# A delta rule, a routed and a dense feed-forward layer in one kernel: fillers by length, low parts on VectorE, one conversion step on ScalarE

## The chip, the cores and the metric

The kernel runs on one core of a Trainium2 chip. The metric is the device time of one execution in microseconds; of three runs of the kernel before the median counts. Engine names in rows: PE is TensorE (PEld its weight loads), DVE is VectorE, ACT is ScalarE, POOL is GpSimd, SP is SyncE, which only issues transfers here.

## What is computed

Three layers follow each other. All sizes are fixed: 4 batches, 8 heads, 768 steps, head size 48; 3072 tokens of 384; 8 experts with 1024 hidden units; a last layer with 2048.

```python
for t in range(S):                       # delta rule, per batch and head
    y[:, :, t] = einsum('bhd,bhde->bhe', q[:, :, t], state)
    v_old = einsum('bhde,bhd->bhe', state, kt)          # kt: normalised key
    state = state + bt * einsum('bhd,bhe->bhde', kt, vt - v_old)
...
h = np.maximum(x[mask] @ w1[e], 0.0)     # tokens of expert e (argmax of cosine logits)
out[mask] = gate_w[mask, None] * (h @ w2[e])
...
h = np.maximum(x @ w_in, 0.0)            # last layer; weights arrive in float64
return (h * h @ w_out)
```

## The kernel before

**Delta rule.** The sequence is cut into 24 steps of 32 positions (`NS`, `C`), four steps to a group. Within a step the recurrence is solved as a triangular system: `gram` multiplies keys with keys on TensorE, and `lanes` (line 191) lists the operations that invert the 32x32 systems of one group on VectorE: a transposition `turned` of 128x1024, a Newton iteration for the norms, factors, `scale`, 31 pairs `mul` and `acc` (lines 263 and 271), and a transposition `end` into `TTl[g]`. The list comes in stages of operations with a cost each, where an operation may cost zero. `Stream` holds one group's list and `fill` hands out its operations three times a step, by cost left and time to the step that needs them, so that VectorE works on later groups between the two `blocks` (line 321) that each step itself needs there: `Ub` and `Wb`. A step runs `mmV`, `mm1K`, `U`, then `W`, then `dS` for the next state; `mm1Q` stands behind `W` in steps 0 to 14 and ahead of it from 15 on, and `gram` of a later step ahead of `W`. In the prologue the first group's solve is interleaved with the first operations of the second group's. `warm(n)` runs n matmuls of 128 columns that write an unused bank. Engines take their instructions in program order, each for itself.

**Experts.** TensorE multiplies in a form with three matmuls: a float32 operand is split into a high part that TensorE's format holds and a low part that remains, and high x high, high x low and low x high are summed (`mm3`, lines 1088 to 1090). Expert e's first layer runs over eight blocks `fb` into three banks in turn (`P1`); ScalarE writes the high part `hh` of the result, VectorE the low part `hl` (line 1139), which frees the bank. The second layer runs over four token tiles in the order 0, 3, 1, 2; ScalarE scales them into `y` (line 1178), for tile 3 VectorE adds two halves (line 1180), and GpSimd stores the rows by an indirect transfer into `x2` (`to_x2`, line 1181), with row numbers that it reads from `xe`. After each block and each tile `run(k, ng, nw)` issues what else is due: `weights` splits the next pieces of weights (`split`, line 576: ScalarE rounds the high part, line 573; VectorE subtracts for the low part in the first ten pieces, GpSimd in nearly all later ones), `ng` operations of `gate` (norm, exponential, reciprocal), and `nw` operations of the queue `q64`. There are ten pieces to an expert: four over 768 columns of its second layer, then six over 512 of the next expert's first; expert 7's six are over 768.

**Conversion.** `q64` holds 28 pieces (12 over 512 columns, 16 over 384) of seven operations each from `w64`: the last layer's float64 weights are read as pairs of 32-bit words and made float32 by integer operations on VectorE (lines 1043 to 1057 and 1046), and each piece is stored into a scratch in DRAM, `wscr`, on SP's queue (line 1047). The last layer loads them back and splits them.

**Last layer.** Eight blocks of 384 tokens, on TensorE throughout.

## Time and profile before

| | us |
|---|---|
| three runs | 1028.61, 1035.83, 1039.15 |
| median | 1035.83 |
| profiled execution, its own time | 1029.11 |
| its span, first to last instruction | 1027.1 |

| stage | from | to | length |
|---|---|---|---|
| prologue | 0 | 52.09 | 52.09 |
| delta steps 0 to 19 | 52.09 | 249.71 | 197.62 |
| steps 20 to 23, last routing | 249.71 | 297.53 | 47.82 |
| expert 0 | 297.53 | 332.37 | 34.84 |
| experts 1 to 7 | 332.37 | 603.80 | 271.43 |
| first block of the last layer, to its last transposition | 603.80 | 637.54 | 33.74 |
| rest of the last layer | 637.54 | 1027.10 | 389.56 |

The stages were set by first matmuls of lines on TensorE. PEclk in a row is the granted clock as a share of 2.4 GHz. A busy VectorE may be one that works or one whose instruction stands; the length of single instructions of one form tells these apart.

### The profile page before, as it was taken

What the parts mean: (1) busy time and instruction counts of PE and PEld (TensorE: products, weight loads), DVE (VectorE), ACT (ScalarE), POOL (GpSimd) and SP (SyncE); (2) the same over time, 40 slices, a digit from 0 to 9 for tenths busy, and PEclk for the clock granted to TensorE, in tenths of its full rate; (3) what the DMA queues carried; (4) which work ended last, traced back from release to release, by engine and by line L of the source; (5) the groups of instructions that cost most, each with busy time, mean ns of one, the idle gap of its engine ahead of it and who ended that gap; (6) DMA issues with size and microseconds to landing.
All of it is one profiled execution on the core that took longest, in us unless ns stands there. A gap on an engine that the chain in (4) does not pass through costs nothing.

```text
span 1027.1 us, 22831 instructions
## 1 busy us (share of the span) xinstructions
PE 936.3 (91%) x9278; PEld 843.4 (82%) x9278; DVE 680.6 (66%) x1563; ACT 431.2 (42%) x1023; POOL 200.5 (20%) x176
## 2 busy tenths in 40 slices
PE   6688889799889889889889799999999999999998
PEld 5576667666677778678768788999999999999998
DVE  6789899998566999999999948160606060606060
ACT  2246566566624443443442446150505050505050
POOL 2000020112321464464464542000000000000000
PEclk9879898899989899999998999999999999999999
DMA  8558442241235663663673453101010000000000
GB/s 312 160 178 265 155 155 92 90 137 62 67 108 181 211 226 123 211 225 127 213 229 114 167 167 114 38 9 35 12 33 14 28 20 28 19 28 20 24 1 24
DMA packets 55443, 113.61 MB, mean 111 GB/s; under 512 B 5955, under 2 KB 34090, under 8 KB 55328
## 3 DMA queue, kind: packets, MB, share of 16 engines
q1 hardware_dynamic: 47600, 96.18, 28.7%
q0 software_dynamic: 3456, 9.59, 2.6%
q10 hardware_dynamic: 4272, 6.28, 1.9%
q8 instruction: 75, 1.23, 0.5%
q14 instruction: 40, 0.33, 0.1%
HBM read 82.02 MB, written 30.79 MB: 110 GB/s over the span
## 4 chain that ended last, share of the span: by engine, by line
PE 48%; DVE 14%; issue 2%; ACT 1%; DMA 1%; POOL 0%; SPq 0%; POOLq 0%; ACTq 0%; DVEq 0%
PE gp L1088 7%; PE gp L1090 7%; PE gp L1089 7%; PE xp L1088 4%; PE xp L1090 4%; PE xp L1089 4%; PE yp L1088 2%; PE yp L1089 2%; PE sp L1088 2%; PE yp L1090 2%; PE sp L1089 2%; PE sp L1090 2%; DVE t2k L1053 2%; DVE t2k L1051 1%; DVE gsm L83 1%
## 5 line engine op out<-in xcount | busy, mean ns | idle before, releaser
L1237 DVE TENSOR_TENSOR t4k<-t2k 128x384 f32<-128x384 f32 x128 | 77.3, 604 | 235.8 <-ACT t2k L1236 234.8
L263 DVE TENSOR_TENSOR tmp<-AL,TL 128x112 f32<-128x112 f32 (+15 forms) x186 | 62.0, 339 | 2.6
L271 DVE TENSOR_TENSOR TL<-TL,tmp 128x112 f32<-128x112 f32 (+15 forms) x186 | 61.7, 338 | 2.6
L1088 PE MATMUL gp<-wb,hh 128*128 128x384 f32 x184 | 63.2, 344 | 0.0
L369 ACT ACTIVATE Sb<-sp 48x384 f32<-48x384 f32 x92 | 44.7, 485 | 43.1 <-PE sp L359 41.6
L1090 PE MATMUL gp<-wb,hl 128*128 128x384 f32 x184 | 62.2, 338 | 0.3 <-DVE hl L1139 0.3
L1089 PE MATMUL gp<-wb,hh 128*128 128x384 f32 x184 | 62.1, 338 | 0.0
L1088 PE MATMUL gp<-xh,W 128*128 128x384 f32 (+1 forms) x153 | 53.8, 352 | 5.3 <-DVE hl L1139 5.0
L1088 PE MATMUL sp<-xh,W 128*128 128x384 f32 (+1 forms) x150 | 53.0, 353 | 4.7 <-DVE hl L1139 3.2
L1088 PE MATMUL yp<-xh,W 128*128 128x384 f32 (+1 forms) x153 | 52.8, 345 | 3.6 <-DVE hl L1139 3.3
L1181 POOL DMA_INDIRECT x<-y,xe x32 | 35.2, 1099 | 105.2 <-ACT y L1178 44.8
L485 POOL DMA_INDIRECT xs<-XG,sloti x24 | 26.8, 1118 | 146.9 <-ACT Ub L331 53.0
L1089 PE MATMUL gp<-xl,W 128*128 128x384 f32 (+1 forms) x153 | 53.4, 349 | 0.0
L1090 PE MATMUL gp<-xh,W 128*128 128x384 f32 (+1 forms) x153 | 53.3, 348 | 0.0
L1089 PE MATMUL yp<-xl,W 128*128 128x384 f32 (+1 forms) x153 | 52.7, 344 | 0.2 <-DVE xl L924 0.2
L1090 PE MATMUL yp<-xh,W 128*128 128x384 f32 (+1 forms) x153 | 52.6, 344 | 0.0
L1089 PE MATMUL sp<-xl,W 128*128 128x384 f32 (+1 forms) x150 | 52.4, 349 | 0.0
L1090 PE MATMUL sp<-xh,W 128*128 128x384 f32 (+1 forms) x150 | 52.3, 348 | 0.0
L1088 PE MATMUL xp<-wb,hh 128*128 128x384 f32 x152 | 51.6, 340 | 0.0
L1089 PE MATMUL xp<-wb,hh 128*128 128x384 f32 x152 | 51.3, 338 | 0.0
L1090 PE MATMUL xp<-wb,hl 128*128 128x384 f32 x152 | 51.3, 338 | 0.0
L359 PE MATMUL sp<-Wb,kL 128*48 128x96 f32 x736 | 45.5, 275 | 2.4 <-issue 1.0
(317 smaller groups left out, 2671.2 us busy)
## 6 DMA issues: line engine op xcount, KB each, us to landing
W<-in_moe_w_dram SPq DMA_DIRECT2D x42, 256.0 KB
W<-in_kq_dram SPq DMA_DIRECT2D x20, 512.0 KB
hb<-in_moe_w_dram SPq DMA_DIRECT2D x24, 384.0 KB
t4k<-in_moe_w_in_dram SPq DMA_DIRECT2D x12, 512.0 KB
t4k<-in_moe_w_out_dram SPq DMA_DIRECT2D x16, 384.0 KB
W<-wscr SPq DMA_DIRECT2D x16, 384.0 KB
xs<-padrow ACTq DMA_DIRECT2D x8, 693.0 KB
xe<-xs SPq DMA_DIRECT2D x8, 594.0 KB
```

The lines of the kernel that those rows point to most:

```text
L83: ops.append(lambda: V.scalar_tensor_tensor(t, t, -0.5, y, ALU.mult, ALU.mult))
L263: V.tensor_tensor(tv[0], AL[:, j, j + 1 :].unsqueeze(1).broadcast_to([128, n, m]), T[:, :n, j : j + 1].broadcast_to([128, n, m]), ALU.mult,)
L271: V.tensor_tensor(T[:, : j + 1, j + 1 :], T[:, : j + 1, j + 1 :], tv[0], ALU.add)
L359: PE.matmul(SP_[hq][64 * par : 64 * par + D, b * 96 : b * 96 + 96], kL2[g][:, i, b * 2 + hq], Wb[hq].rearrange("p b (m r) e -> p b r m e", ...
L369: A.activation(Sb[hq][r : r + D, :, :, par, :], SP_[hq][r : r + D, 0:384].rearrange("p (b m e) -> p b m e", b=4, m=2), AF.Copy,)
L485: G.indirect_dma_start(out=xs, out_offset=bass.IndirectOffsetOnAxis(ap=si[:, i : i + 1].bitcast(U32), axis=0), in_=XG[g][:, i0 + i, :], in ...
L1053: lambda: V.scalar_tensor_tensor(v["a"], u.bitcast(U32), float(0x70200000), v["a"], ALU.is_ge, ALU.mult),
L1088: PE.matmul(ps, hs, rh, start=first, stop=False)
L1089: PE.matmul(ps, hs, rl, start=False, stop=False)
L1090: PE.matmul(ps, ls, rh, start=False, stop=last)
L1181: to_x2 = lambda e=e, n=n, t=t, y=y: G.indirect_dma_start(out=x2, out_offset=bass.IndirectOffsetOnAxis(ap=xe[e][:n, t, XT : XT + 1].bitcas ...
L1237: V.tensor_tensor(s2, r, r, ALU.mult)
```

## The change

In the delta rule: each operation costs 0.075 us and its elements over 960, each transposition is split into four of 128x256 at a cost of 0.55, and a stream is one list without stages. `fill` gives each of the first two streams its due by the length left and the time left. The first solve runs alone; the second stream starts with step 0. `mm1Q` always stands ahead of `W`, `gram` behind it, the four masks of group 0 behind `W` of step 0, and the shares of the three fillers are 0.25, 0.4 and 0.35. `warm` matmuls are 512 columns wide and fewer: 29 in place of 146 before the loop, 10 in place of 55 in step 0, 2 in place of 10 in steps 1 to 3.

In the experts: every low part goes to VectorE. Conversion has six operations: the shift of line 1052 goes, the comparison uses an absolute value that ScalarE makes in place, and comes last. Its store goes to GpSimd's queue. Fewer conversion operations are popped (5 in the eight blocks of experts 1 to 6 in place of 8, and 6, 6, 4 at the tiles in place of 7, 7, 6; for expert 0 6, 6, 4 in place of 5, 5, 4). The exponential in `gate` is padded with empty operations so that it starts a group of four and its reader comes in the next. Row numbers are copied to a tile `rows` of their own.

```diff
-def add(f, n=C, gap=0.12):
-    ops.append((0.065 + n / 960 + gap if n else 0.0, f))
+def add(f, n=C, c=None):
+    ops.append((0.075 + n / 960 if c is None else c, f))
-def turned():
-    V.transpose(AL, GPs[g].rearrange("p s h j -> p j (s h)"))
+def turned(j):
+    V.transpose(AL[:, j : j + 8], GPs[g][:, :, :, j : j + 8].rearrange("p s h j -> p j (s h)"))
+
+def turn():
+    for j in range(0, C, 8):
+        add(lambda j=j: turned(j), c=0.55)
...
-    first, ops = ops, []
-    add(turned, C * C)
+    turn()
...
-    add(turned, C * C)
+    ops.append((0.0, begin))
+    turn()
-    for n, o in enumerate(nw):
-        add(o, C if n < 2 else 0)
-    first, ops = ops, []
+    for o in nw:
+        add(o)
...
-def end():
-    TTl[g] = wp.tile([128, C, C], F32, name="TTt", bufs=2)
+def end(i):
+    if i == 0:
+        TTl[g] = wp.tile([128, C, C], F32, name="TTt", bufs=2)
+    V.transpose(
+        TTl[g].rearrange("p u i -> p i u")[:, i : i + 8], T.rearrange("p c i -> p i c")[:, i : i + 8]
+    )
...
-if g == 0:
-    for u in range(1, 4):
-        ops.append((0.0, lambda u=u: vh(u)))
-third, ops = ops, []
-if g:
-    ops, third = third, ops
-add(end, C * C)
-return [o for o in (first, second, third, ops) if o]
+            add(lambda u=u: masked(g, u), 256)
+for i in range(0, C, 8):
+    add(lambda i=i: end(i), c=0.55)
+return ops
-    split(wbuf[i], c, raw.shape[1], raw, A, V if nstep < 10 or nstep > 78 and nstep % 2 else G)
+    split(wbuf[i], c, raw.shape[1], raw, A, V)
...
-        c, f = self.stages[0].popleft()
+        c, f = self.ops.popleft()
-        return c
+        self.due -= c
-    streams[:] = [st for st in streams if st.stages]
-    act = [[st, st.left / max((4 * st.g - now) / part, 1), len(st.stages)] for st in streams[:2]]
-    if len(act) == 2:
-        act[1][1] = min(act[1][1], max(1.2 * part, 4 * part - act[0][1]))
-    while act or route_q:
-        for a in act:
-            a[1] -= a[0].pop()
-        act = [a for a in act if a[1] > 0 and len(a[0].stages) == a[2]]
+    streams[:] = [st for st in streams if st.ops]
+    for st in streams[:2]:
+        st.due += st.left * min(1.0, part / max(4 * st.g - now, part))
+    while True:
+        act = [st for st in streams[:2] if st.ops and st.due > 0]
+        for st in act:
+            st.pop()
         if route_q:
             route_q.popleft()()
-    streams[:] = [st for st in streams if st.stages]
+        elif not act:
+            break
-        PE.matmul(YP[:, :128], ones, tri, start=True, stop=True)
+        PE.matmul(YP, ones, tri.unsqueeze(1).broadcast_to([128, 4, 128]), start=True, stop=True)
-warm(34)
+warm(9)
-grams(0, 1, 0, 4, 9)
+grams(0, 1, 0, 4, 0)
-while len(st0.stages) > 2:
+for _ in range(26):
...
-grams(1, 2, 0, 4, 9)
+warm(4)
+grams(1, 2, 0, 4, 2)
-grams(0, 2, 4, 8, 5)
+grams(0, 2, 4, 8, 1)
...
-nxt = Stream(1)
-nn = 0
-while len(st0.stages) > 2 or len(st0.stages) == 2 and len(st0.stages[0]) > 28:
+while st0.ops:
     st0.pop()
-while st0.stages:
-    st0.pop()
-    if len(nxt.stages) > 2 and nn % 3 == 0:
-        nxt.pop()
-    nn += 1
-grams(0, 2, 8, 12, 5)
+grams(0, 2, 8, 12, 1)
 drain(route_q)
-streams.append(nxt)
-for b in range(4):
-    masked(0, b)
+streams.append(Stream(1))
...
-    fill(s, 0.2)
+    fill(s, 0.25)
+    if s < 4:
+        warm(2 if s else 10)
+    mm1Q(s)
     if s > 0:
         xT = xrt(s - 1)
-    early = s >= 15
+    while g not in TTl or streams and streams[0].g == g and streams[0].ops:
+        streams[0].pop()
+    W(s, 0)
+    W(s, 1)
+    if s == 0:
+        for b in range(4):
+            masked(0, b)
     if ahead < min(15 if s < 4 else NS, s + 12):
-        early = False
         gram(ahead)
         ahead += 1
-    if early:
-        mm1Q(s)
-    while g not in TTl:
-        streams[0].pop()
-    if s < 4:
-        warm(10 if s else 55)
-    W(s, 0)
-    W(s, 1)
     if scats:
-    fill(s + 0.2, 0.4)
+    fill(s + 0.25, 0.4)
...
-    if not early:
-        mm1Q(s)
...
-        streams[-1].pop()
-    fill(s + 0.6, 0.4)
+    fill(s + 0.65, 0.35)
...
+ops.extend([lambda: None] * (-(len(ops) + 1) % 4))
 add(lambda: A.activation(lg, lg, AF.Exp))
+ops.extend([lambda: None] * 3)
...
+def top():
+
+    V.scalar_tensor_tensor(v["ai"], v["h"], -0x40000000, ui, ALU.bitwise_and, ALU.bitwise_or)
+
+def low():
+
+    V.scalar_tensor_tensor(u, v["l"].bitcast(U32), 2.0**-52, u, ALU.mult, ALU.mult)
+    A.activation(v["h"].bitcast(F32), v["h"], AF.Abs)
+
 def end():
-    V.tensor_tensor(v["a"], v["a"], u, ALU.add)
-    nc.sync.dma_start(wscr[i][:, c * n : (c + 1) * n], v["a"])
+    V.scalar_tensor_tensor(v["a"], v["h"].bitcast(F32), float(0x38100000), v["a"], ALU.is_ge, ALU.mult)
+    nc.gpsimd.dma_start(wscr[i][:, c * n : (c + 1) * n], v["a"])
 return [
     begin,
-    lambda: V.scalar_tensor_tensor(v["ai"], v["h"], -0x40000000, ui, ALU.bitwise_and, ALU.bitwise_or),
-    lambda: V.tensor_scalar(ui, v["h"], 1, None, ALU.logical_shift_left),
-    lambda: V.scalar_tensor_tensor(
-        v["a"], u.bitcast(U32), float(0x70200000), v["a"], ALU.is_ge, ALU.mult
-    ),
+    top,
     lambda: V.tensor_scalar(ui, v["ai"], -0x800000, None, ALU.bitwise_and),
-    lambda: V.scalar_tensor_tensor(u, v["l"].bitcast(U32), 2.0**-52, u, ALU.mult, ALU.mult),
+    low,
+    lambda: V.tensor_tensor(v["a"], v["a"], u, ALU.add),
     end,
...
+    rows_e = mp.tile([128, 4], I32, name="rows", bufs=2)
+    gops.insert(0, lambda e=e, rows_e=rows_e: V.tensor_copy(rows_e, xe[e][:, :, XT].bitcast(I32)))
...
-            run(fb + 1, 4, 2 if e + 1 == E else 1)
+            run(fb + 1, 4, 2 if e + 1 == E else (1, 1, 0, 1, 0, 1, 0, 1)[fb])
...
-            out_offset=bass.IndirectOffsetOnAxis(ap=xe[e][:n, t, XT : XT + 1].bitcast(U32), axis=0),
+            out_offset=bass.IndirectOffsetOnAxis(ap=rows_e[:n, t : t + 1].bitcast(U32), axis=0),
...
-        run(9 + i, 0, (7, 7, 6, 0)[i] if e else (5, 5, 4, 0)[i])
+        run(9 + i, 0, (6, 6, 4, 0)[i])
```

## Rows read from the trace of the kernel before

**Rows 1.** Busy time by stage: us from:to, length, then each engine; PEclk; DMA.

```profile
52.09:249.71 197.62, 171.94 (x3727) 134.80 (x3726) 184.03 (x580) 115.83 (x326) 23.39 (x28) 0.89 0.43 142
...
297.53:332.37 34.84, 32.85 (x173) 28.55 (x174) 24.77 (x59) 17.09 (x35) 2.56 (x2) 1.00 0.62 199
332.37:603.80 271.43, 241.04 (x1193) 207.52 (x1193) 249.55 (x411) 116.13 (x236) 141.77 (x98) 0.94 0.57 183
603.80:637.54 33.74, 31.49 (x176) 29.36 (x177) 25.26 (x37) 20.11 (x42) 9.68 (x6) 1.00 0.46 149
637.54:1027.10 389.56, 385.98 (x2223) 385.44 (x2221) 131.35 (x253) 125.52 (x276) 1.90 (x1) 1.00 0.07 22
```

**Rows 2.** Waits from 332.37 to 603.80 us: who <- whom: us, times, longest.

```profile
PE gp L1088 <- DVE hl L1139: 12.6, 3, 5.0
...
PE yp L1088 <- DVE hl L1139: 9.0, 4, 5.3
...
PE sp L1088 <- DVE hl L1139: 7.4, 3, 3.2
```

**Rows 3.** Timelines of VectorE and GpSimd in expert 4: start, length, what.

```profile
450.16 0.36 DVE L1056 TENSOR_SCALAR W<-t2k 128x384 int32<-128x384 int32 x1
450.56 0.56 DVE L1057 SCALAR_TENSOR_TENSOR W<-t4k,W 128x384 f32<-128x384 uint32 x1
451.15 2.01 DVE L1046 TENSOR_TENSOR t2k<-t2k,W 128x384 f32<-128x384 f32 x1
...
457.64 1.75 DVE L81 TENSOR_TENSOR gsm<-gsm 128x4 f32<-128x4 f32 x1
...
463.38 0.16 DVE L83 SCALAR_TENSOR_TENSOR gsm<-gsm 128x4 f32<-128x4 f32 x1
...
450.21 1.18 POOL L1181 DMA_INDIRECT x<-y,xe  x1 [1.89 <-ACT y L1178]
451.42 1.32 POOL L576 TENSOR_TENSOR W<-W 128x512 fp32r<-128x512 f32 x1
455.35 5.78 POOL L576 TENSOR_TENSOR W<-hb,W 128x768 fp32r<-128x768 f32 x3 [2.62 <-ACT W L573]
```

**Rows 4.** Line 576 alone, busy time in the same stretch: DVE, then POOL.

```profile
332.37:603.80 271.43, 1.29 (x2) 111.01 (x69) 0.94 0.57 183
```

**Rows 5.** VectorE's groups in expert 0: xcount | busy, mean ns | idle before.

```profile
L576 DVE TENSOR_TENSOR W<-hb,W 128x768 fp32r<-128x768 f32 x3 | 2.9, 955 | 1.2 <-ACT W L573 1.1
L576 DVE TENSOR_TENSOR wb<-W,wb 128x512 fp32r<-128x512 f32 x4 | 2.6, 689 | 1.3 <-ACT wb L573 1.2
...
L924 DVE TENSOR_TENSOR W<-ch,W 128x448 fp32r<-128x448 f32 x2 | 1.2, 620 | 3.0 <-ACT W L923 3.0
...
L1052 DVE TENSOR_SCALAR W<-t4k 128x512 int32<-128x512 int32 x2 | 0.9, 426 | 0.1
...
L1057 DVE SCALAR_TENSOR_TENSOR W<-t4k,W 128x512 f32<-128x512 uint32 x1 | 0.7, 684 | 0.0
```

**Rows 6.** Line 1181, the indirect stores of `y`: from issue to landing.

```profile
DMA to landing us min/median/max: 2.0/3.4/7.2
```

**Rows 7.** Timeline of VectorE, prologue and step 0.

```profile
40.17 1.95 DVE L203 STREAM_TRANSPOSE AL<-GPs 128x1024 f32<-128x1024 f32 x1 [4.25 <-ACT GPs L173]
...
53.95 1.43 DVE L188 TENSOR_TENSOR PL<-PL,mask 128x256 f32<-128x256 f32 x4
55.26 0.99 DVE L321 TENSOR_TENSOR Ub<-ch,blk 128x768 f32<-128x768 f32 x1
```

**Rows 8.** Timeline of TensorE, prologue and step 0.

```profile
15.02 0.43 PE L153 MATMUL sp<-W 64*32 64x32 f32 x21 [2.79 <-issue]
...
21.77 0.68 PE L153 MATMUL ch<-W 64*32 64x32 f32 x40 [2.98 <-issue]
...
55.11 4.08 PE L680 MATMUL yp<-tri,ones 128*128 128x128 bf16 x55
```

**Rows 9.** Waits from 332.37 to 603.80 us, GpSimd's longest on ScalarE's rounding.

```profile
POOL W L576 <- ACT W L573: 29.9, 10, 5.4
```

More of the change, by code (lines that the diff above doesn't have):

```diff
@@ L219, in factors @@
             add(lambda: V.reciprocal(r, nl))
-            add(lambda: V.tensor_tensor(r, r, r, ALU.mult), 0)
-            add(lambda: V.tensor_tensor(gam, r, betaL[:, g], ALU.mult), 0)
-            add(lambda: V.tensor_scalar(t1, gam, -1.0, None, ALU.mult), 0)
+            add(lambda: V.tensor_tensor(r, r, r, ALU.mult))
+            add(lambda: V.tensor_tensor(gam, r, betaL[:, g], ALU.mult))
+            add(lambda: V.tensor_scalar(t1, gam, -1.0, None, ALU.mult))
         nw = []
@@ L271, in acc @@
             V.tensor_tensor(T[:, : j + 1, j + 1 :], T[:, : j + 1, j + 1 :], tv[0], ALU.add)
-        def end():
-            TTl[g] = wp.tile([128, C, C], F32, name="TTt", bufs=2)
-            V.transpose(TTl[g].rearrange("p u i -> p i u"), T.rearrange("p c i -> p i c"))
-        v_steps = (23, 25, 27, 29) if g else (23,)
+        def end(i):
[4 more added lines that the diff above has]
+            )
         for j in range(31):
             for f in (mul, acc):
-                add(lambda f=f, j=j: f(j), (31 - j) * (j + 1), 0.02)
-            if j in v_steps:
-                u = v_steps.index(j)
-                add(lambda u=u: vh(u), 384, 0.02)
+                add(lambda f=f, j=j: f(j), (31 - j) * (j + 1))
+            if j in (23, 25, 27, 29):
+                u = (j - 23) // 2
+                add(lambda u=u: vh(u), 384)
                 if g:
-                    add(lambda u=u: masked(g, u), 256, 0.02)
-        if g == 0:
-            for u in range(1, 4):
-                ops.append((0.0, lambda u=u: vh(u)))
-        third, ops = ops, []
-        if g:
-            ops, third = third, ops
-        add(end, C * C)
-        return [o for o in (first, second, third, ops) if o]
+                    add(lambda u=u: masked(g, u), 256)
+        for i in range(0, C, 8):
+            add(lambda i=i: end(i), c=0.55)
+        return ops
     def mmV(s, hq):
@@ L648, in __init__ @@
             def __init__(self, g):
-                self.g, self.stages = g, [deque(ops) for ops in lanes(g)]
-                self.left = sum(c for ops in self.stages for c, _ in ops)
+                self.g, self.ops = g, deque(lanes(g))
+                self.left, self.due = sum(c for c, _ in self.ops), 0.0
             def pop(self):
-                c, f = self.stages[0].popleft()
+                c, f = self.ops.popleft()
                 f()
                 self.left -= c
-                if not self.stages[0]:
-                    self.stages.pop(0)
-                return c
+                self.due -= c
         def fill(now, part):
-            streams[:] = [st for st in streams if st.stages]
-            act = [[st, st.left / max((4 * st.g - now) / part, 1), len(st.stages)] for st in streams[:2]]
-            if len(act) == 2:
-                act[1][1] = min(act[1][1], max(1.2 * part, 4 * part - act[0][1]))
-            while act or route_q:
-                for a in act:
-                    a[1] -= a[0].pop()
-                act = [a for a in act if a[1] > 0 and len(a[0].stages) == a[2]]
+            streams[:] = [st for st in streams if st.ops]
[5 more added lines that the diff above has]
+                    st.pop()
                 if route_q:
                     route_q.popleft()()
-            streams[:] = [st for st in streams if st.stages]
+                elif not act:
+                    break
         def queue(fs):
```

7 lines of the change are left out of this document (2 added, 5 removed).

## Prediction

> **What bounds the kernel now.** I read the windows by stage first, since each stage has its own limit [rows 1]. The last stage, from 637.54 us, is TensorE alone: busy 385.98 of 389.56 us at granted clock 1.00. The change leaves it as it is, so nothing is to be had there. The seven experts 1 to 7 (332.37 to 603.80, 38.8 us each) look different from expert 0 just ahead of them: expert 0 takes 34.84 us with TensorE busy 32.85 at clock 1.00 and GpSimd at 2.56; the seven have TensorE busy 34.4 each at clock 0.94, VectorE busy 249.55 of 271.43 (0.92), and GpSimd 141.77. The arithmetic of TensorE is nearly the same in all eight, so the seven are 7 x 32.85 = 230 us of matmuls in 271 us.
>
> Where the other 41 us lie, the waits of that stretch tell: TensorE stands for 29.0 us, in ten waits of up to 5.3 us, until VectorE has written `hl` [rows 2]; the rest, some 11 us, is that matmuls after such a stop run at the lower of the two clock levels (1.2 and 2.4 GHz), as the mean of 0.94 against expert 0's 1.00 shows. So VectorE is late. Why it is late, the timeline shows [rows 3]: an addition over 128x384 takes 2.01 us while GpSimd runs its subtraction over 512 columns (1.32 us), and operations over 128x4 take 1.75 us while GpSimd runs three subtractions in a row (5.78 us); the same 128x4 form takes 0.16 us when GpSimd is still. While GpSimd only issues an indirect store (450.21, 1.18 us), VectorE's two operations beside it take their usual 0.36 and 0.56. It is the subtractions, then, 69 of them with 111.01 us in this stretch [rows 4], that hold VectorE, and much of VectorE's 0.92 is standing still.
>
> The delta loop is the other stage that the change touches: steps 0 to 19 take 197.62 us with VectorE busy 184.03 [rows 1]. There VectorE truly works, and only less work, or the 13.6 us between, can shorten it.
>
> **Experts: low parts.** Per expert VectorE gets ten subtractions: six over 512 columns at 0.69 and four over 768 at 0.955 [rows 5], 8.0 us. What it has without GpSimd's hold I take from expert 0, which does its own low parts on VectorE: 24.77 us busy [rows 1], eight of them in the stretch. To make a later expert of it: plus the two missing over 512 (1.4); minus the splitting of the first `x`, which only expert 0 has (3 x 0.62 = 1.9) [rows 5]; plus conversion work. Expert 0 holds ten operations of it, a whole piece and three of the next (two of L1052, one of L1057) [rows 5]. The change leaves 28 pieces x 6 = 168 operations and pops 5 + 16 = 21 per expert: eleven more. An operation costs 0.43 or 0.68 over 512 columns [rows 5] and 0.36 or 0.56 over 384 [rows 3]; with two of the cheap and four of the dear kind and 12 wide and 16 narrow pieces that is 3.2 us a piece, 0.53 an operation, 5.8 us. Sum: 24.8 + 1.4 - 1.9 + 5.8 = 30.1 us.
>
> TensorE needs 32.85. So it becomes the bound, with VectorE at 0.9 of its time. In order on VectorE, a low part now waits for ScalarE's rounding. In expert 0 that cost 2.5 us over seven of them [rows 5], 0.36 each, so 3.6 for ten: 33.7. I take 33.6 us for experts 1 to 6; from below 32.85, from above the first rival. Expert 7 has no next `x` to split (-1.8), but 26 conversion operations (+2.7) and low parts that are all 768 wide (+1.6): 32.6, and most of it in its first half, where it pops two operations a block. There it will hold TensorE again; I take 35.5, between 33 and today's 38.8. Together 6 x 33.6 + 35.5 = 237.1 against 271.43: **-34.3** (from -41.5, all at 32.85, to the rivals below).
>
> **Experts: the rest.** The dropped shift (L1052) is in the count. The new absolute value runs on ScalarE; no row shows that function. ScalarE's 236 instructions of the stretch take 0.49 us each and fill 116.13 of 271.43 [rows 1]; 3.5 more per expert are hidden in its idle time. So nothing below, and above the wait of the first rival, which I put there. The placement of the exponential takes a possible VectorE wait out of the path; I count nothing. The copied row numbers cost one 0.16 us operation and let the next load of `xe` go before the last store has been issued; hidden under a whole expert.
>
> The 28 stores move from SP's queue to GpSimd's. On SP they stood in front of loads and waited for VectorE; on GpSimd's queue they stand in front of the indirect stores and the token index near the end of expert 7, which have time: without subtractions GpSimd is left with a few issues of about 1.2 us. What an issue of a plain store costs there no row shows; below nothing, above the 1.18 us of the indirect one [rows 3], 28 x 1.18 = 33 us spread over an engine that loses 111.
>
> On the path the move can cost one thing. The stored tiles `t2k` have two buffers, and `ht` takes one of them in each expert; with three and a half pieces to an expert, in every other one of experts 1 to 6 a piece begins in the second layer in the buffer of the piece just stored, and VectorE stands until the store has landed. An indirect store takes 3.4 us from issue to landing in the median [rows 6]; behind the standing piece waits line 1180, which frees the bank that the fourth tile needs, and TensorE feels what exceeds its reserve of one bank. No row shows a plain store from this queue. I take **+3** for three experts, from 0 to 10.
>
> One rule speaks against this move: the Trainium skill, "SBUF — State Buffer", section "SBUF: two separate sides", says that a DMA issued from GpSimd's queue has its descriptors written by GpSimd and stands while VectorE runs a two-port operation. By it a store waits out a 0.36 or 0.43 us operation of VectorE; in the trace an issue beside a 0.36 us operation still took 1.18 us [rows 3], and no store is issued there yet. By the row the sum gets nothing; by the rule 28 x 0.43 = 12 us of waits on GpSimd, which has that time, so nothing either unless the last store is late for its reload.
>
> **Start of the last stage** (603.80 to 637.54): 33.74 us with TensorE busy 31.49 [rows 1]. Five of its subtractions move to VectorE, which is busy 25.26. **-1** of at most 2.2.
>
> **Prologue.** Today the first block `Ub` starts at 55.26 [rows 7]. Ahead of it on VectorE lie, and go elsewhere: a wait of 4.25 us with the second group's transposition behind it (1.95) [rows 7], nine more operations of that group (1.4 at 0.16), and four masks (1.43) [rows 7]: 9.0. Splitting two transpositions adds: a quarter costs between 0.49 (a quarter of 1.95) and 0.65 (that plus a small operation's 0.16); I take 0.55, so 0.25 each, 0.5 in all. VectorE would be there 8.5 us sooner. TensorE must be too. It stands at 15.02 and at 21.77 for 2.79 and 2.98 us for nothing that the profile names [rows 8], 127 matmuls apart, and 146 warming matmuls become 29, of four times the width: about 117 matmuls fewer, nearly one such stretch, so one wait of 2.9 less, and up to some 5 us of matmuls less at 0.074 each and more where the clock is low (55 take 4.08 us) [rows 8]. So between -2.9 and -8.5; I take **-7**.
>
> On that distance the Trainium skill, "Runtime: NRT & Kernel Launch", section "Instruction fetch mechanics", says that instructions are fetched in blocks of 256 and that the crossing of a boundary is mostly hidden. The distance agrees (127 matmuls, each with its weight load, are 254 instructions); "hidden" doesn't, since TensorE stands 2.8 us. By that section the prologue would gain the matmuls' time only, some 5 us in place of 7.
>
> **Delta loop.** What left the prologue comes back here, where VectorE is the bound: the transposition and nine operations 3.3, the masks 1.4, and ten split transpositions at 0.25, 2.5 (0 to 6.5). Step 0 wins about 1: its 55 warming matmuls hold TensorE to 59.19 [rows 8]. An even spread of the fillers can't make less work of it; of the 13.6 us idle I give it 0.5 (0 to 4). Sum **+5.7**, and with the prologue **-1.3** (-10 to +8). In groups: steps 0 to 3 now carry one solve in 4 steps and one in 8, and should be the longest, steps 5 to 15 near 10 us each.
>
> **Sum.** Span 1027.10 - 34.3 + 3 - 1.0 - 1.3 = 993.5; the profiled execution took 1029.11, 2.0 more than its span: 995.5. The three timed runs lie from 1028.61 to 1039.15 with the median 6.7 above the profiled one, so I go a little up: **998 us**.
>
> **Rivals.**
> *VectorE waits for ScalarE* (slower). Each low part, and the last step of each conversion, now waits in VectorE's own line, while ScalarE stands behind a `y` that waits for TensorE. GpSimd waited 29.9 us in ten waits for the same rounding, 3.0 each [rows 9]. If the four low parts of the second layer cost that and the other six 0.36, VectorE needs 30.1 + 12 + 2.2 = 44.3 per expert, +39 us for the experts, about 1067. It decides from 8.7 us of waits per expert (0.87 a low part); between 0.36 and that lies a lesser gain, around 1014. For it: the order of the line. Against: expert 0, which has this order already, shows 0.36, and 4 to 6 conversion operations lie queued at each tile to fill the time. 0.04 for slower, 0.10 for the middle.
> *The hold stays* (slower). If VectorE's long operations have another cause, its 35.7 us per expert get 8.0 more and lose 7 conversion operations (3.7): 39.9, at today's share of 0.92 43.4 per expert, +32, about 1062. It decides when over 0.57 of the 9.8 us by which 39.9 exceeds 30.1 remain. The Trainium skill, "Perfetto Trace Analysis", section "Optimizing Scalar/DVE Operations", would have a saturated VectorE give work to others, GpSimd perhaps, and warns that these two share a read port. The change goes the other way; the rows side with the warning [rows 3]. 0.03.
> *The delta loop takes its whole upper bound* (+8 in place of -1.3): about 1007. For it: VectorE is full there and gets more. 0.12.
> My forecast has the other 0.71.
>
> **Chances.** About 1% (10 us) is what a measurement of this kernel can tell. Faster by more: the forecast, the third rival and half of the middle, 0.88; within it the other half, 0.05; slower 0.07. The range goes from 977 (995.5 with experts, stores, prologue and loop at their lower ends: 7.2, 3 and 8.7 less) to 1016 (just past the middle case).
>
> **What would show it.** Right: in experts 1 to 7 no subtraction on GpSimd, 128x4 operations at 0.16 throughout, clock 1.00, spacing near 33.6, VectorE busy near 30, `Ub` of step 0 near 48. Wrong: VectorE idle before L576 by more than 0.9 a time, TensorE's waits on `hl` still above 2 us an expert in 1 to 6, VectorE waiting for a store of `wscr` for over 5 us in an expert, or steps 0 to 19 over 206 us.

## The result and the profile after

The changed kernel takes 986.94 us (median of 4, 985.13 to 992.41) against 1033.78 (median of 4) beside it: a ratio of 0.9594, 95% interval 0.9553 to 0.9635. Ratios, here and below, are estimated from the executions that didn't fall into a slower state, and so are not always the quotient of the two medians. Its profiled execution took 985.13 us with a span of 983.40, 43.7 less than the span before. The prediction was 998 with a range of 977 to 1016, so the time lies within it, 11 us under the forecast.

Busy time by stage after, the stretches that answer to [rows 1] (from:to, length, then each engine's busy time with its instructions, PEclk, DMA):

```profile
48.13:247.51 199.38, 169.92 (x3657) 127.29 (x3656) 186.24 (x618) 117.08 (x326) 20.29 (x25) 0.89 0.42 137
294.23:328.84 34.61, 32.71 (x172) 28.38 (x173) 26.64 (x62) 16.48 (x34) 3.03 (x4) 1.00 0.62 198
328.84:526.35 197.51, 195.12 (x1033) 169.09 (x1033) 166.53 (x385) 110.03 (x227) 38.63 (x45) 1.00 0.64 213
526.35:564.66 38.31, 32.81 (x161) 27.27 (x161) 30.40 (x71) 18.67 (x37) 8.03 (x11) 0.96 0.61 202
564.66:597.50 32.84, 30.20 (x175) 28.96 (x175) 24.94 (x44) 21.55 (x43) 2.33 (x2) 1.00 0.46 146
597.50:983.40 385.90, 382.12 (x2224) 381.57 (x2222) 129.66 (x253) 124.41 (x275) 0.00 (x0) 1.00 0.07 22
```

Expert 7 alone in the kernel before:

```profile
565.03:603.80 38.77, 32.35 (x161) 28.09 (x161) 29.00 (x51) 17.32 (x33) 21.99 (x15) 0.96 0.50 167
```

The delta loop is 199.38 us long (197.62 before) with VectorE busy 186.24 (184.03). Experts 1 to 6 take 32.9 us each, with TensorE busy 195.12 of 197.51 at clock 1.00, which is expert 0's pace and a little better. Expert 7 alone still falls behind (38.31 against 38.77, clock 0.96 in both).

The rest of the last layer, from the same matmul on, takes 385.90 us in place of 389.73. TensorE is the limit there in both kernels, at clock 1.00, with as many matmuls, but its last 2223 matmuls take 382.1 us in the ten profiles of kernels with the changed experts' part, whatever their low parts and stores do, and 386.1 in the four with the part as before. So neither the low parts nor the stores nor the delta rule's part does it. Which of the other changes does was not tried and stays open.

| from | to | before | after | difference |
|---|---|---|---|---|
| start | first `Ub` | 55.26 | 50.71 | -4.55 |
| first `Ub` | `Ub` of step 20 | 196.87 | 198.32 | +1.45 |
| `Ub` of step 20 | tile 3 of expert 0 | 67.25 | 66.98 | -0.27 |
| tile 3 of expert 0 | tile 3 of expert 7 | 272.43 | 235.81 | -36.62 |
| tile 3 of expert 7 | end | 435.29 | 431.58 | -3.71 |
| sum | | 1027.10 | 983.40 | -43.70 |

(Tile 3 stands for the first matmul on an expert's fourth token tile, which is the second in the order of its second layer.) TensorE's ten waits of 29.0 us for `hl` [rows 2] are gone: from 328.84 to 526.35 none of its matmuls waits for `hl` (weight loads do, by 0.5 us at most), and one waits 1.4 us for a low part. The lines that answer to [rows 3] and [rows 5], VectorE in expert 4 after, where the four low parts over 768 columns run on it:

```profile
434.87 0.96 DVE L573 TENSOR_TENSOR W<-hb,W 128x768 fp32r<-128x768 f32 x1
435.75 0.36 DVE L1047 TENSOR_SCALAR W<-t2k 128x384 int32<-128x384 int32 x1
436.01 0.17 DVE L76 TENSOR_SCALAR gsm<-gsm 128x4 int32<-128x4 int32 x1
436.21 0.16 DVE L78 TENSOR_TENSOR gsm<-magic,gsm 128x4 int32<-128x4 int32 x1
436.41 0.16 DVE L81 TENSOR_TENSOR gsm<-gsm 128x4 f32<-128x4 f32 x1
436.49 0.61 DVE L1133 SCALAR_TENSOR_TENSOR hl<-yp,hh 128x448 fp32r<-128x448 f32 x1
437.02 0.95 DVE L573 TENSOR_TENSOR W<-hb,W 128x768 fp32r<-128x768 f32 x1
```

The 128x4 operations that took 1.75 us now take 0.16 throughout, and GpSimd beside them issues an indirect store and a plain one, and nothing else:

```profile
434.66 0.99 POOL L1175 DMA_INDIRECT x<-y,rows  x1 [3.91 <-ACT hh L1132]
447.40 0.57 POOL L1042 DMA_DIRECT2D wscr<-t2k  x1 [11.74 <-DVE gate L871]
```

### The profile page after: what moved, and what is told of

Its sections match the earlier page's. It is cut to its first block, busy times and chain, and to the rows that moved or that the text cites. A ratio compares the mean times of both kernels' runs of the same rounds, so it can differ in the third digit from the quotient of the medians.

```text
span 983.4 us, 22409 instructions
## 1 busy us (share of the span) xinstructions
PE 913.2 (93%) x9092; PEld 808.0 (82%) x9092; DVE 628.3 (64%) x1653; ACT 444.4 (45%) x1051; POOL 94.6 (10%) x130
## 3 DMA queue, kind: packets, MB, share of 16 engines
q1 hardware_dynamic: 43568, 89.89, 27.8%
## 5 line engine op out<-in xcount | busy, mean ns | idle before, releaser
L1231 DVE TENSOR_TENSOR t4k<-t2k 128x384 f32<-128x384 f32 x128 | 71.4, 558 | 230.8 <-ACT t2k L1230 230.1
L271 DVE TENSOR_TENSOR TL<-TL,tmp 128x175 f32<-128x175 f32 (+15 forms) x186 | 60.3, 336 | 2.5
L263 DVE TENSOR_TENSOR tmp<-AL,TL 128x31 f32<-128x31 f32 (+15 forms) x186 | 60.2, 335 | 2.1
L366 ACT ACTIVATE Sb<-sp 48x384 f32<-48x384 f32 x92 | 44.7, 486 | 29.7 <-PE sp L356 28.2
L1082 PE MATMUL gp<-xh,W 128*128 128x384 f32 (+1 forms) x153 | 52.0, 340 | 0.0
L1080 PE MATMUL gp<-xh,W 128*128 128x384 f32 (+1 forms) x153 | 51.9, 339 | 0.0
L1080 PE MATMUL sp<-xh,W 128*128 128x384 f32 (+1 forms) x150 | 51.0, 340 | 0.8 <-ACT t2k L1230 0.8
L1082 PE MATMUL sp<-xh,W 128*128 128x384 f32 (+1 forms) x150 | 51.0, 340 | 0.0
L337 PE MATMUL ch<-Ub,TTt 128*32 128x192 f32 x384 | 22.8, 351 | 26.7 <-DVE Ub L318 26.7
L1175 POOL DMA_INDIRECT x<-y,rows x32 | 34.9, 1089 | 131.4 <-ACT y L1172 53.9
```

Of the source, the lines that this page charges most:

```text
L263: V.tensor_tensor(tv[0], AL[:, j, j + 1 :].unsqueeze(1).broadcast_to([128, n, m]), T[:, :n, j : j + 1].broadcast_to([128, n, m]), ALU.mult,)
L271: V.tensor_tensor(T[:, : j + 1, j + 1 :], T[:, : j + 1, j + 1 :], tv[0], ALU.add)
L337: PE.matmul(CH[hq][C * f : C * f + C, 256:448], TTl[g][:, i * 8 + hq * 4 + f], Ub[hq][:, f].rearrange("p b e -> p (b e)"), start=True, sto ...
L366: A.activation(Sb[hq][r : r + D, :, :, par, :], SP_[hq][r : r + D, 0:384].rearrange("p (b m e) -> p b m e", b=4, m=2), AF.Copy,)
L1080: PE.matmul(ps, hs, rh, start=first, stop=False)
L1082: PE.matmul(ps, ls, rh, start=False, stop=last)
```

## Experiments on the experts

One measure serves all of them, from the profile of each kernel: the distance from tile 3 of expert 0 to tile 3 of expert 7, the busy time of two engines in it, and the time that VectorE was held. An instruction counts as held if it takes at least 0.6 us more than the shortest of its form and one of GpSimd's operations of `split` runs meanwhile; held time is that excess, summed over experts 1 to 7. The last column has the number of such instructions and how many of them took over 4 us. In the kernels with such operations no instruction was that late without one.

| kernel | distance | VectorE busy | GpSimd busy | in `split`, GpSimd | held | instructions held, over 4 us |
|---|---|---|---|---|---|---|
| before | 272.43 | 255.59 | 136.51 | 111.7 | 93.2 | 65, 0 |
| before, delta rule's part changed | 274.54 | 258.65 | 135.91 | 111.2 | 94.1 | 61, 1 |
| before, low parts on VectorE | 246.42 | 213.72 | 32.57 | 0 | 0 | 0 |
| before, copies on GpSimd | 243.58 | 200.23 | 79.18 | 53.1 | 26.5 | 14, 2 |
| after | 235.81 | 200.27 | 47.16 | 0 | 0 | 0 |
| after, stores on SP | 236.34 | 200.75 | 31.48 | 0 | 0 | 0 |
| after, low parts on GpSimd | 312.76 | 251.21 | 144.41 | 107.0 | 103.3 | 38, 8 |
| the same, stores on SP | 288.05 | 247.09 | 131.73 | 107.3 | 100.9 | 50, 5 |

**The low parts alone.**

```diff
-            split(wbuf[i], c, raw.shape[1], raw, A, V if nstep < 10 or nstep > 78 and nstep % 2 else G)
+            split(wbuf[i], c, raw.shape[1], raw, A, V)
```

> The kernel before with the one line changed: all low parts on VectorE, conversion, queue and delta loop as before. Theory (the hold was the whole of it): VectorE 35.7 - 14 + 8.0 = 30 us per expert, TensorE the bound at 32 to 33, clock 1.00 in experts 1 to 7: 36 us gained, 994 to 999 us. Rival (the lighter conversion is needed too, since seven operations more per expert keep VectorE full): spacing near 35.5, about 1014 us.

Measured: 995.3 us against 1028.63. The ratio, 0.9638 (0.9540 to 0.9735), is that of three executions (986.59, 991.39 and 999.22), 37 us under the kernel before; the fourth, which was profiled, took longest (1001.59), with its experts at clock 0.99.

```profile
317.50:563.92 246.42, 232.62 (x1193) 199.01 (x1192) 213.72 (x490) 115.96 (x239) 32.57 (x29) 0.99 0.62 203
357.83:530.14 172.31, 165.71 (x861) 141.35 (x860) 150.95 (x348) 82.45 (x172) 23.23 (x20) 1.00 0.63 206
```

The first theory's time, or a little better, but in the one profile a part of the rival's mechanism: there the line is worth 26.0 of the 36.6 us, and experts 2 to 6 are 34.5 us apart where the changed kernel has 32.4. VectorE is busy 150.95 of 172.31 (0.88) with 28 conversion operations an expert, and TensorE 165.71. In that execution the other 10 us would be the rest of the experts' part, perhaps the lighter conversion (VectorE has 2.6 us less an expert in the changed kernel). The other three executions say otherwise: they are within 5 us of the changed kernel (0.9638 against 0.9594), and 4 of these lie in the last layer, so there the line alone may be worth nearly the whole. They have no profile, and the split stays open. With the subtractions left on GpSimd the lighter conversion gains nothing, as the next two runs show.

**The low parts back on GpSimd**, everything else as changed (the diff above, the other way).

> The changed kernel with one thing undone: the low parts of experts 1 to 7 and five of the last stage are subtracted on GpSimd again. Theory (GpSimd's subtraction holds VectorE): VectorE loses 8.0 us of subtractions per expert and gets back about 14 us of standing still (100 us over seven experts before), so 27.0 - 8.0 + 14 = 33 busy beside TensorE's 32: spacing of experts 1 to 6 near 35 us instead of 32.5, expert 7 near 40, and the start of the last stage 2 longer; about 1008 us (1003 to 1022). Rival (the lighter conversion and its spread alone did it): spacing stays 32.5 and the time stays within 4 us of the changed kernel's 987.

Measured: 1063.28 us (1.032, 1.0233 to 1.0407), 55 over the theory, 41 over its upper end, and slower than before. Taking this one line back costs 75 us beside the changed kernel with its stores on SP, run in the same group (988.24); adding it alone gained 37. The theory had priced the hold by its total, and the total came as expected (103.3 us). What it missed stands in the timeline of VectorE, then of GpSimd and TensorE, in expert 4 of this kernel:

```profile
474.15 0.17 DVE L76 TENSOR_SCALAR gsm<-gsm 128x4 int32<-128x4 int32 x1 [0.34 <-ACT junk L859]
474.35 9.07 DVE L78 TENSOR_TENSOR gsm<-magic,gsm 128x4 int32<-128x4 int32 x1
...
474.00 1.00 POOL L1175 DMA_INDIRECT x<-y,rows  x1 [2.77 <-PE yp L1082]
475.03 1.30 POOL L573 TENSOR_TENSOR W<-W 128x512 fp32r<-128x512 f32 x1
476.29 5.35 POOL L573 TENSOR_TENSOR W<-hb,W 128x768 fp32r<-128x768 f32 x3
481.61 1.79 POOL L573 TENSOR_TENSOR W<-lb,W 128x768 fp32r<-128x768 f32 x1
...
484.20 0.74 PE L1080 MATMUL yp<-xh,W 128*128 128x448 f32 x1 [6.86 <-DVE hl L1133]
```

One operation over 128x4 is held for 9.07 us, until the last of five GpSimd subtractions in a row ends at 483.40; the writing of `hl` stands behind it, and TensorE waits 6.86 us. Before, the four subtractions from 455.35 us on [rows 3] held four operations of VectorE one after another, and `hl` got through between them. VectorE in the kernel before, at that place:

```profile
455.79 1.82 DVE L78 TENSOR_TENSOR gsm<-magic,gsm 128x4 int32<-128x4 int32 x1
...
459.42 1.73 DVE L83 SCALAR_TENSOR_TENSOR gsm<-gsm 128x4 f32<-128x4 f32 x1
461.07 0.61 DVE L1139 SCALAR_TENSOR_TENSOR hl<-yp,hh 128x448 fp32r<-128x448 f32 x1
461.61 1.33 DVE L84 SCALAR_TENSOR_TENSOR gsm<-gsm 128x4 f32<-128x4 f32 x1
```

**The same with the stores on SP.**

```diff
-            nc.gpsimd.dma_start(wscr[i][:, c * n : (c + 1) * n], v["a"])
+            nc.sync.dma_start(wscr[i][:, c * n : (c + 1) * n], v["a"])
```

> The changed kernel with the low parts back on GpSimd, as in the run that took 1063 us, and the 28 stores back on SP's queue as well. Theory (in that run a store stood on GpSimd's queue until VectorE had made its tile, the subtractions piled up behind it into runs, and each run held VectorE as a whole): without the stores on that queue the spacing of experts 1 to 6 falls from 44 to 35 or 36 us, 1005 to 1018 us. Rival (the conversion's step on ScalarE and the fewer operations per expert do the harm, whatever the queue): spacing stays over 41, 1045 to 1065.

Measured: 1037.39 us (1.0104, 1.0016 to 1.0192), a time between the two, and a spacing of 41.2 in experts 1 to 6 (44.5 with the stores on GpSimd), at the rival's edge. Beside the changed kernel with its stores on SP (988.24) the line now costs some 50 us. The queue explains 24.7 of the 40.3 us by which the distance grew over that of before (GpSimd waits there for VectorE to make the tile and the subtractions bunch behind it). The remaining 15.6 are not the queue. They stand with 50 holds, of which five are over 4 us, where before had none over 3 (the kernel with before's experts and the changed delta rule had one of 7.26):

```profile
455.58 0.62 DVE L1133 SCALAR_TENSOR_TENSOR hl<-sp,hh 128x448 fp32r<-128x448 f32 x1 [1.07 <-ACT hh L1132]
456.12 8.63 DVE L1047 TENSOR_SCALAR W<-t2k 128x384 int32<-128x384 int32 x1
464.67 0.16 DVE L76 TENSOR_SCALAR gsm<-gsm 128x4 int32<-128x4 int32 x1
```

The held total is much the same in all four kernels that subtract on GpSimd, 93 to 103 us for 107 to 112 us of subtractions; what differs is whether it comes in pieces that TensorE's three banks cover or whole. The four longest holds of this kernel (8.48, 8.63, 8.92 and 9.05 us) have one thing in common with the 9.07 above: the run of subtractions begins directly behind an indirect store on GpSimd, with its inputs ready, where the run that let VectorE through began after a wait for ScalarE. The traces of these four kernels bear this out: of their runs of three or more subtractions with under 0.3 us between them, the 12 that began within 0.03 us of a transfer's issue on GpSimd (nine indirect stores, three plain ones) each held one operation of VectorE for 4.6 us or more, and the 15 that began after a wait of 0.35 us or more held none over 2.4. Why the two engines take turns in the one case and not in the other stays open; a run without the issue ahead wasn't tried.

**Copies in place of subtractions**, in the kernel before:

```diff
+        if El is G:
+            G.tensor_copy(part(wt, 1, c, n), raw)
+        else:
+            El.tensor_tensor(part(wt, 1, c, n), raw, hi.bitcast(F32), ALU.subtract)
-        El.tensor_tensor(part(wt, 1, c, n), raw, hi.bitcast(F32), ALU.subtract)
```

> The kernel before, where GpSimd's low parts are replaced by a plain copy of the raw weights on GpSimd (one input in place of two); the low parts of those weights are left out of the computation, everything else stands. Theory (what holds VectorE is GpSimd's operation on two inputs): VectorE's 128x4 operations stay at 0.16 us beside the copies, the 14 us of standing still per expert go, experts 1 to 7 near 33 us each, 992 to 1000 us. Rival (any GpSimd operation over 512 or 768 columns holds VectorE): 128x4 operations of over 1 us remain, 37 to 39 us per expert, 1022 to 1034.

Measured: 993.55 us (0.9677, 0.9577 to 0.9777), the theory's time, but the reason is not clean. GpSimd's groups and two lines of VectorE's timeline:

```profile
L577 POOL CAST W<-W 128x512 fp32r<-128x512 f32 (+1 forms) x21 | 15.2, 723 | 26.5 <-DMA W<-in_moe_w_dram 11.6 <-DMA W<-wscr 8.2 <-PE sp L1093 6.5
L577 POOL CAST wb<-hb 128x768 fp32r<-128x768 f32 x12 | 9.5, 826 | 0.0
...
407.36 0.57 DVE L81 TENSOR_TENSOR gsm<-gsm 128x4 f32<-128x4 f32 x1
407.97 3.55 DVE L83 SCALAR_TENSOR_TENSOR gsm<-gsm 128x4 f32<-128x4 f32 x1
```

Copies hold VectorE too (3.55 us beside four copies over 768), 26.5 us in 14 instructions, but they take 53.1 us in place of 111.7 and hold for half of that instead of five sixths. So it isn't a second input alone; less time on GpSimd is part of the gain.

**The stores on SP, low parts on VectorE** (the diff of the stores above, in the changed kernel).

> The changed kernel with its 28 stores on SP's queue again. Theory (the queue of the store matters little, because VectorE waited 1.8 us in all for landed stores and SP's loads are issued far ahead): within 2 us of the changed kernel's 987. Rival of the prediction (+3 of waits for buffers on GpSimd's queue): 2 to 4 us less, 983 to 985. Rival (a store on SP that waits for VectorE holds the loads of weights behind it): TensorE waits for weights, 3 to 10 us more.

Measured: 988.24 us; the distance is 0.5 us longer than the changed kernel's. With VectorE at 0.85 of its time in the experts, the queue of the stores is worth nothing. The waits that the store on GpSimd's queue causes in the changed kernel, and its transfers:

```profile
L1042 POOL DMA_DIRECT2D wscr<-t2k x28: 539/575/763, 322.8 to 561.3; - x28
  DVE t2k L1204: 3.1, 1
  DVE t2k L1143: 1.6, 1
  DVE t2k L1033: 0.2, 1
DMA to landing us min/median/max: 2.1/4.7/7.4
```

The longest of them (L1204) stands in the start of the last stage, where TensorE waits 1.5 us behind it; with the stores on SP it is 1.6, and from tile 3 of expert 7 to the end the two kernels take 431.6 and 431.8.

## Experiments on the prologue and the delta loop

**The delta rule's part alone**, in the kernel before (the hunks of `lanes`, `Stream`, `fill`, `warm`, the prologue and the order of a step).

> The kernel before with the delta rule's part of the change alone (split transpositions, spread by length, first solve alone, warming matmuls of 512 columns). Theory (from the two traces, block of step 20 reached 3.1 us sooner, the rest untouched): 3 us less than the kernel before, 1029 to 1032 beside a median of 1033.8. Rival (the sum of the prediction as made, gains in the prologue given back in the loop): within 1.3 us of before. Rival (the experts start from another state of the queues and lose): over 1036.

Measured: 1032.07 us against 1028.63 (1.0037, 1.0002 to 1.0073, ten runs): 0 to 7 us slower, not 3 faster. The first theory took one pair of profiles at its word. Over all the profiles the block of step 20 begins at 247.57, 249.89 and 252.13 us in the three kernels with the old loop (mean 249.9) and at 248.46, 249.03, 249.29, 249.30, 250.17, 252.22 and 253.49 in seven with the new one (mean 250.3). Equal delta loops differ by 5 us there, and the change is worth nothing that these can tell. The first block comes 4.0 us sooner (54.5 to 50.6 in the mean) and the loop gives it back, which is the first rival's account, though not its time.

**Warming matmuls cut in four, and left out.**

```diff
-            for _ in range(n):
-                PE.matmul(YP, ones, tri.unsqueeze(1).broadcast_to([128, 4, 128]), start=True, stop=True)
+            for _ in range(4 * n):
+                PE.matmul(YP[:, :128], ones, tri, start=True, stop=True)
```

> The changed kernel with its warming matmuls cut in four of 128 columns: as many columns, three matmuls more for each, 87 more before the first block of step 0. Theory (TensorE's unnamed stops come every 127 matmuls, whatever their width, 16 us of them in the first 50): 87/127 of a stop more and 2 us of small-matmul overhead, first block 2 to 5 us later, at 53 to 56 us. Rival (columns set the time): first block within 0.7 us of 50.7.

```diff
-        warm(4)
-        grams(1, 2, 0, 4, 2)
+        grams(1, 2, 0, 4, 0)
...
-        grams(0, 2, 4, 8, 1)
+        grams(0, 2, 4, 8, 0)
...
-        grams(0, 2, 8, 12, 1)
+        grams(0, 2, 8, 12, 0)
```

> The changed kernel without the 20 warming matmuls of 512 columns between the Gram products of the prologue (the nine ahead of them and those of steps 0 to 3 stand). Theory (TensorE's own time, with the stops, sets the first block now, since VectorE had the first solve ready 6 us before): 9 us of warming go, some 4 come back at the lower clock, first block 4 to 6 us sooner, at 45 to 47 us, VectorE's first solve (44.7) being next. Rival (the stops set it alone and swallow what the matmuls give up): first block not before 49.5 us.

Measured: first block at 52.72 us cut in four, between the two expectations, and at 49.50 without the 20, the rival's value: some 10 us of matmuls left out brought 1.2 (seven executions with the changed prologue lie from 50.16 to 51.32; these two kernels have one execution each). TensorE's stops after 127 matmuls, first in the changed kernel, then without the warming:

```profile
13.93 0.70 PE L153 MATMUL gp<-W 64*32 64x32 f32 x42 [3.71 <-issue]
19.81 0.76 PE L153 MATMUL sp<-W 64*32 64x32 f32 x49 [1.27 <-issue]
26.78 0.81 PE L153 MATMUL ch<-W 64*32 64x32 f32 x54 [3.25 <-issue]
40.29 1.18 PE L153 MATMUL ch<-W 64*32 64x64 f32 x64 [3.89 <-issue]
45.22 0.37 PE L153 MATMUL sp<-W 64*32 64x64 f32 x2 [2.12 <-issue]
```

```profile
13.92 0.70 PE L153 MATMUL gp<-W 64*32 64x32 f32 x42 [3.68 <-issue]
20.54 0.71 PE L153 MATMUL sp<-W 64*32 64x32 f32 x43 [5.01 <-issue]
26.68 0.73 PE L153 MATMUL ch<-W 64*32 64x32 f32 x44 [4.53 <-issue]
41.07 0.94 PE L153 MATMUL ch<-W 64*32 64x64 f32 x46 [4.66 <-issue]
45.60 0.97 PE L153 MATMUL gp<-W 64*32 64x64 f32 x48 [2.47 <-issue]
```

Counted from the first matmul these are the same five places, after 223, 350, 477, 858 and 985 matmuls in both (a sixth, after 731, and without the warming a seventh, after 604, are left out here). The stops grow by what the warming gives up (15.7 us in all with it, 23.9 without), and the moments at which TensorE goes on hardly move. So it is less TensorE's work that times the prologue than when its next 127 matmuls become available; that this is a fetch behind the loads of the same moments is likely, since the trace lists 16 KB transfers of kind "instruction" on a queue of their own there, but it wasn't tried. More matmuls, though shorter ones, came out later; whether far fewer would help no run tells.

## Two versions made from this

**Work for VectorE's wait.** It has the first solve ready at 44.7 us and stands 5.98 us for TensorE:

```profile
50.71 0.96 DVE L318 TENSOR_TENSOR Ub<-ch,blk 128x768 f32<-128x768 f32 x1 [5.98 <-PE ch L307]
```

```diff
         streams.append(Stream(1))
+        got = 0.0
+        while got < 5.0:
+            c0 = streams[0].left
+            streams[0].pop()
+            got += c0 - streams[0].left
+        streams[0].due = 0.0
```

> The changed kernel, in which VectorE takes the first 5 us of the second group's solve before the first block of step 0, while it waits 6 us there for TensorE. Theory (VectorE's work bounds the delta loop, so work done in that wait is gained): first block still at 50 to 51, steps 0 to 3 together 5 us shorter (54.4 to 49.5), block of step 20 near 245, 982 us. Rival (the operations stand in line ahead of the first block and hold it, or the steps' length is set by the chain of a step and not by the fillers): block of step 20 unchanged at 249 to 253, 986 to 990.

**Expert 7 relieved.**

```diff
-                    run(fb + 1, 4, 2 if e + 1 == E else (1, 1, 0, 1, 0, 1, 0, 1)[fb])
+                    run(fb + 1, 4, 1)
```

> The changed kernel with the conversion spread otherwise: one operation in each of the eight blocks of the first layer in experts 1 to 6 (24 an expert in place of 21), so that 8 in place of 26 are left for expert 7. Theory (expert 7 is the only one where VectorE, with 26 operations, holds TensorE; experts 1 to 6 have 5 us of VectorE's time to spare): expert 7 33 us in place of 36.6, experts 1 to 6 unchanged at 32.5, 984 us. Rival (a piece then begins elsewhere, and waits for a buffer of t2k or for ScalarE eat it up): experts 1 to 6 33 or more, 987 to 990.

> Both of these in one kernel. Theory: the gains add, since one lies in the delta loop and the other in the experts: 979 us, 8 us less than the changed kernel. Rival (one of the two gives nothing): 982 to 985, and the trace shows which.

The changed kernel again, beside them:

> The changed kernel itself once more, beside the three versions of this group: 985 to 990 us, first block of step 0 at 50 to 51 us, block of step 20 between 249 and 253.5 (the scatter that kernels with this same delta loop have shown), tails of experts 1 to 6 32.5 us apart and expert 7 36.6.

Measured in one group, against 1026.76 us for before: the changed kernel again 984.42 (0.9596, 0.9559 to 0.9634), the first version 978.70 (0.9541, 0.9500 to 0.9582), the second 984.98 (0.9608), both 979.76 (0.9566, 0.9527 to 0.9605). The changed kernel came 0.6 us under what was expected. The first version does most of what the theory said: steps 0 to 3 take 49.3 us in place of 53.2, and the block of step 20 begins at 246.93 us, and at 243.40 in the kernel with both, sooner than in any of the seven with the new loop above. These lines now fill the wait:

```profile
44.41 2.04 DVE L203 STREAM_TRANSPOSE AL<-GPs 128x256 f32<-128x256 f32 x4
...
50.76 0.94 DVE L211 TENSOR_TENSOR AL<-AL,sm 128x248 f32<-128x248 f32 x3
51.62 0.95 DVE L318 TENSOR_TENSOR Ub<-ch,blk 128x768 f32<-128x768 f32 x1
```

The second is a case of the rival, at the theory's time. Experts 2 to 6 and expert 7 in it, and then in the changed kernel again:

```profile
354.76:521.69 166.93, 163.43 (x862) 140.83 (x861) 145.59 (x337) 91.36 (x190) 32.75 (x40) 1.00 0.65 217
521.69:554.94 33.25, 31.04 (x161) 26.64 (x160) 27.83 (x66) 17.86 (x37) 6.46 (x8) 1.00 0.55 188
```

```profile
351.02:513.05 162.03, 161.78 (x862) 141.22 (x861) 139.20 (x323) 90.78 (x188) 33.07 (x38) 1.00 0.64 214
513.05:549.72 36.67, 31.11 (x161) 26.77 (x160) 32.16 (x73) 19.71 (x39) 8.03 (x10) 0.99 0.67 222
```

Expert 7 gets its 3.4 us, but the five others lose 4.9 and expert 1 another 1.65: VectorE goes from 139.20 to 145.59 us, 0.87 of its time, and TensorE, which had 161.78 of 162.03, now stands for 3.5. The spare time that I had counted there (5 us an expert) is not there to be used; whether the share or the places of the three more operations do it, these runs don't tell. The gain reaches further than expert 7: from tile 3 of expert 7 to the end the second is 5.2 us shorter (427.97 against 433.16), so in the stages that it touches it is 2.0 us ahead, less than equal delta loops differ by. The kernel with both meets its theory's 979 us, but by the first version's gain alone: the second adds nothing that the times show. The best kernel of these runs is the first version, 5.7 us under the changed one by medians, with intervals that still touch.

## Why the prediction held, step by step

**What bounds it: right.** VectorE was late because GpSimd's subtractions held it, and in a lesser part by its own conversion work: with the subtractions gone its busy time in the experts fell by 42 us (by 55 with the lighter conversion) while it took over 8 us of work an expert. The hold returns with them.

**Low parts, -34.3, and stores, +3: right in kind, 4 us short.** The seven experts take 235.8 us in place of 271.4. Four terms were mis-sized. VectorE's 30.1 us an expert came out as 27.8 in experts 1 to 6: the base from expert 0 held 0.9 us of small operations that only that expert has, and I added durations of rows, while neighbours overlap by up to a tenth of a microsecond each, which the windows count once (the rows sum to 30.7 in the changed kernel). The 3.6 us of waiting for ScalarE were 2.7 (16.2 us of idle time before L573 in six experts, 0.27 each, of which ScalarE's rounding ended 10.5), and I let them lengthen TensorE's time, while they lie in VectorE's slack: TensorE set the pace (195.12 of 197.51 us busy), at 32.9 instead of 33.6. The stores cost 0.2 us in experts 1 to 6. And expert 7's 35.5 was 38.3, hardly less than before: a wait of 1.6 for a landed store came there, TensorE then stood 3.7 for `ht`, and it stood for `hl` besides. The working put the whole gain under the low parts; the run with that line alone bears this out by its times and for 26.0 us by its one profile, so what the lighter conversion adds, whose relief is inside my 5.8 us for 11 operations, stays open.

**Start of the last stage, -1: about right. The rest of the last layer, put at nothing: -3.8.** From tile 3 of expert 7 to the end the profile has -3.7: the end of expert 7 takes 0.8 us more, the start 0.7 less (32.84 against 33.57), and the rest 3.8 less. I had said that the change leaves that stage as it is and nothing is to be had there. Its matmuls got 1% quicker, for a reason that stays open, and this part of the gain is luck.

**Prologue, -7: -4.55, and -4.0 over all profiles.** VectorE's side was right: it was ready for `Ub` 10.5 us sooner (8.5 worked out). The step that failed is TensorE's, "one wait of 2.9 less" for 117 matmuls fewer. Its unnamed stops add up to 15.7 us, where before had 14.6: the warming had filled time in which TensorE would have stood anyway. The Trainium skill, "Runtime: NRT & Kernel Launch", section "Instruction fetch mechanics", takes the crossing of an instruction block as mostly hidden; here stops of 1.3 to 3.9 us stand at six places, 127 matmuls or twice that apart, and the prologue goes by them.

**Delta loop, +5.7: +4.4 over all profiles.** Steps 0 to 3 became the longest (16.8, 13.1, 12.5, 12.3) and steps 5 to 15 lie near 10, as said. From the first `Ub` to that of step 20 the two profiles of the table above differ by 1.45 us, but the three with the old loop take 195.3 in the mean (193.1 to 196.9) and the seven with the new one 199.7 (198.2 to 203.3): what left the prologue comes back here. The terms were a little too dear: four quarters of a transposition take 2.04 us together against 1.95 for one [rows 7], so splitting one costs 0.09 and not 0.25, and a part was met by VectorE's idle time (in the pair its busy time rose from 183.2 to 187.5 us and its idle time fell from 13.7 to 10.8). With the prologue I had -1.3; the profiles have +0.4, and the run of the delta rule's part alone 0 to +7 on the time, which is inside the bounds given (-10 to +8) and on the other side of the value taken.

**A little up, +2.5: not there.** The profiled execution lies 1.8 us under its median, not 6.7.

Of what was to show it right, the 128x4 operations, the clock, VectorE's share and the spacing came as named or better, and `Ub` 2.7 us late; none of the four signs against it came.

The rivals: VectorE did not wait for ScalarE (0.27 us a low part, its point was 0.87), and the hold did not stay; the delta loop with the prologue stayed near nothing, not at +8. As a warning the rival of the hold was worth more than its 0.03: the run with the subtractions back landed at 1063, near its 1062, by bunching rather than by another cause of the hold.

## What to carry to other kernels

Before giving GpSimd two-input work beside a busy VectorE, count its time twice: here VectorE lost 0.83 to 0.97 us for each of GpSimd's (0.5 beside copies), and the loss came at times in one piece of 9 us that stopped TensorE behind it. An edit's price depends on its neighbours (the same line was worth 37 us alone, some 50 in the changed kernel with its stores on SP, and 75 with the stores on GpSimd), so do it alone and undo it before crediting it. Lay the stretches before and after between the same instructions, the ones that should not move too: here the last layer moved. A stage of short matmuls may be timed by the arrival of its instructions; look for stops that keep their moments when the work between them is removed, and give the engine that waits meanwhile something of the next stage.

## What the runs showed of the chip

A VectorE operation of 0.16 us was held for 9.07 us by five GpSimd subtractions in a row. The Trainium skill, "SBUF — State Buffer", section "SBUF: two separate sides", says that the port pair the two engines share (VectorE for some of its operations) goes to whichever begins first for a whole instruction while the other blocks; the kernel before agrees (one VectorE instruction held for about one subtraction, 65 for 69), the two runs with the subtractions back don't, where it went on over four or five instructions. The same section's warning of stores on GpSimd's queue beside VectorE shows in no run: a plain store was issued in 0.54 to 0.76 us there with VectorE busy 0.84 of the time, and landed after 4.7 us in the median (4.8 from SP's queue). That equal programs differ by 5 us in the delta loop, and that splitting a transposition in four costs 0.1 us, were not expected either.
